# Attention scores of the last three query tiles: four fp32 quadrant products, or three rounded products with 128 queries as weights

## The chip, the cores and the metric

The program runs on one core of a Trainium2 chip. The metric is device time in microseconds (us), the median of several executions; one further execution was recorded by the hardware profiler, and all rows below come from that one.

## The reference

Talking-heads attention feeds two dense two-layer networks, all in fp32. The part that the change touches is the product of queries and keys in the second line.

```python
B, H, S, D = 2, 12, 448, 64
scores = 0.125 * q @ k.T                               # per batch and head, 448 x 448
scores = einsum('bhij,hg->bgij', scores, w_pre)        # heads mixed before the softmax
scores = scores - max(scores, -1)
attn = exp(scores); attn = attn / (sum(attn, -1) + 1e-9)
attn = einsum('bhij,hg->bgij', attn, w_post)           # heads mixed after it
x = (attn @ v) as 896 rows of 768
h = x @ w_in;  x = where(h > 0, h, exp(min(h, 0)) - 1) @ w_out
h = x @ w2_in; out = (h * sigmoid(h)) @ w2_out
```

## The kernel before

**Scores.** The 896 query rows of both batches stand in seven tiles of 128 rows (T = 0 to 6). For a tile and a pair of heads p (0 to 5), `qk_pair(T, p)` on PE multiplies queries `qt` (64 partitions for the even head, 64 for the odd one) with keys `kt`. It issues four products, one for each quadrant of the array: head e of the pair picks the rows of the array, half c of the queries picks the columns. Operands are plain fp32, and the trace has two records of a product, each preceded by a weight load. The results lie in two PSUM banks (`pq`, tags qk0 and qk1), one for each head. `qk_evac` scales them into `s`, the even head on ACT and the odd one on DVE.

**Steps.** Attention then runs in 45 hand-ordered steps (`step(s)`). A step mixes heads for 20 query rows: DMAs on SP bring score rows into `blk` (three buffers, two steps ahead); PE makes `pre` from it (`premix`, quadrants of 64x64); DVE takes the row maximum `nmx`; ACT makes `pe` by an exponential with row sums; DVE inverts the sums; POOL scales the second mixing matrix by them into `krn` (`recip`); and in the step after, PE makes `post` (`postmix`, quadrants again), which ACT and DVE copy into `a`. PE's order in a step is `pre`, then in some steps two pairs of `av` (attention times values, 128 rows by 64 columns of the array), then one pair of scores `pq`, then `post` of the step before. Steps with `av` are called long here, the others short. Tables (`QK_AT`, `X_AT`, `D_AT`, `A_AT`, `M_AT`, `B_AT`) say in which step and at which place of it further work is issued; every engine works through its queue in the order in which the code issues.

Scores of tile 4 are made in steps 17 to 22, of tile 5 in 23 to 28, of tile 6 in 29 to 34. Of these 18 steps the eight 17, 19, 21, 25, 27, 29, 31 and 33 are short and the other ten long. Step 17 begins at 66.61 us of the trace, step 18 at 68.93, step 19 at 73.21, step 28 at 103.51, step 29 at 108.69, step 35 at 128.54.

**Weights of the first network** are already prepared in these steps: the table `EARLY` gives for four half chunks the steps of load, `scale_w` (ACT), two bit operations `bits_w` (DVE), the rounding `split_hi` (ACT, a cast to fp32r) and the remainder `split_lo` (DVE). The two networks follow from about 160 us on: every factor there is split into a rounded part (fp32r) and a remainder, and a product is made of three rounded products, high by high, high by low, low by high, with 128x128 weights and 448 columns.

Of the kernel before, what the change touches and what calls it, by code (L numbers as in the profile page):

```python
# [7 lines left out]
F32 = mybir.dt.float32  # L8
F32R = mybir.dt.float32r
# [4 lines left out]
ALU = mybir.AluOpType  # L14
# [3 lines left out]
P = 128  # L18
B, H, S, D = 2, 12, 448, 64
# [3 lines left out]
NP = H // 2  # L23
# [5 lines left out]
HS = 64  # L29
# [6 lines left out]
KO = (0, 2, 4, 1, 3, 5)  # L36
AHEAD = 2
KS = 10
OUT2 = ((0,), (1,), (2,), (0, 1), (3,), (2, 3), (4,), (5,), (4, 5))
KB = -(-S // BI)  # L40

# [37 lines left out]
def attn_moe_moe(ctx: ExitStack, tc: tile.TileContext, q, k, v, w_pre, w_post, w1i, w1o, w2i, w2o, out):  # L79
    nc = tc.nc  # L80
# [3 lines left out]
    def pool(name, **kw):  # L84
        cm = tc.tile_pool(name=name, reuse_waits="tile", **kw)
        return cm, cm.__enter__()

    cm_c, cp = pool("const", bufs=1, side="left")
    cm_k, kp = pool("kt", bufs=1, side="right")
    cm_al, al = pool("align", bufs=1, side="right")  # L90
    al.tile([P, 40], F32, name="align")
    cm_w, wp = pool("qt", bufs=1, side="right")
# [17 lines left out]
        return min(TI, S - t * TI)  # L110

    NQ = len(QTILES)
    qT, kT = {}, {}

    def load_q(T, eng=None, parts=(slice(0, NP),)):
        if T not in qT:
            qT[T] = wp.tile([P, NP, 2 * P], F32, name=f"qt{T}", tag="qT", bufs=3).rearrange("p a b -> p (a b)")[:, :NP * P].rearrange("p (a b) -> p a b", a=NP)
        for p in parts:
            (eng or nc.sync).dma_start(qT[T][:, p], q[T, :, p])

    def load_k(b, p, eng=nc.sync):
        if b == 0:
            kT[p] = kp.tile([P, 2, S], F32, name=f"kt{p}", tag=f"kT{p}")
        eng.dma_start(kT[p][:, b], k[b, p])  # L124

    def load_v(b, g, eng=nc.sync):

# [11 lines left out]
    def qk_pair(T, p, where=("qk0", "qk1")):  # L139

        bs = QTILES[T][1]
        if T not in smap:
            smap[T] = (sp1, sp0, sp2)[T % 3].tile([P, H, S], F32, name=f"s{T}", tag="s")
        pq = [ps.tile([P, S], F32, name=f"pq{T}_{p}_{e}", tag=w, bufs=1) for e, w in enumerate(where)]
        for c in range(2):
            for e in range(2):
                half = slice(e * D, (e + 1) * D)
                nc.tensor.matmul(pq[e][HS * c:HS * c + HS], qT[T][half, p, HS * c:HS * c + HS], kT[p][half, bs[c % len(bs)]], start=True, stop=True, tile_position=(e * D, HS * c))  # L148
        sev.append((T, p, pq))

    def qk_evac(e):
        for T, p, pq in sev:
            o = smap[T][:, 2 * p + e]
            if e == 0:
                nc.scalar.activation(o, pq[0], AF.Copy, scale=0.125)  # L155
            else:
                nc.vector.tensor_scalar(o, pq[1], 0.125, None, op0=ALU.mult)
        if e == 1:
            sev.clear()
# [97 lines left out]
    def av_pair(T, p):  # L257

        b, t = tiles[T]
        m = rows(t)  # L260
        if p % 2 == 0:
            late = T + 1 == len(tiles)
            avt[T] = ps.tile([P, 2, TI], F32, name=f"av{T}_{p}", tag=("pre2", "qk0", "pre0")[p // 2] if late else {(0, 0): "qk0", (0, 2): "qk0", (2, 4): "pre2", (6, 2): "qk0"}.get((T, p), "av"), bufs=1)
        for j in range(4):
            for e in range(2):
                h = 2 * p + e
                nc.tensor.matmul(avt[T][e * D:(e + 1) * D, p % 2, :m], vall[b][:NV, h, j], amap[T][:NV, j * H + h, :m], start=j == 0, stop=j == 3, tile_position=(0, e * D))  # L267
        if p % 2 == 1:
            (xsp if T + 2 >= len(tiles) else xev).append((T, p - 1, m, avt.pop(T)))
# [11 lines left out]
    def av_split():  # L281
        for T, p, m, av in xsp:
            c = slice(tiles[T][1] * TI, tiles[T][1] * TI + m)
            x = x1_tile()
            nc.scalar.copy(x[:, p:p + 2, 0, c], av[:, :, :m])
            nc.scalar.copy(xmap[1][:, p:p + 2, c], av[:, :, :m])
            nc.vector.tensor_tensor(x[:, p:p + 2, 1, c], av[:, :, :m], x[:, p:p + 2, 0, c], op=ALU.subtract)
        xsp.clear()
# [3 lines left out]
    for p in range(NP):  # L292
        load_k(0, p)
        if p < 2:
            load_q(0, nc.scalar, (slice(0, 2), slice(2, NP))[p:p + 1])
# [14 lines left out]
    for p in range(NP):  # L310
        qk_pair(0, p, BANKS[p % 3])
        qk_evac(0)
        qk_evac(1)
    for s in range(AHEAD):
        relayout(s)
    for p in range(LEAD):
        qk_pair(1, p, BANKS[p])
        qk_evac(0)
        qk_evac(1)

    NT_ = len(tiles)
    QK_AT, X_AT, D_AT, A_AT = {}, {}, {}, {}

    def at(d, step, f):
        d.setdefault(int(step), []).append(f)

    for T, n0 in enumerate((-LEAD, 1, 11, 17, 23, 29), 1):
        for p in range(LEAD if T == 1 else 0, NP):
            at(QK_AT, n0 + p, lambda T=T, p=p: qk_pair(T, p))
    for T, st in ((3, 7), (4, 15), (5, 20)):  # L330
        at(D_AT, st, lambda T=T: load_q(T))
    at(A_AT, 26, lambda: load_q(6, nc.scalar))
    AV_AT = (8, 10, 12, 14, 16, 18, 20, 22, 23, 24, 26, 28, 30, 32, 34, 36, 38, 40, 42, 43, 44)
    for T in range(NT_ - 1):
        for p in range(NP):
            at(X_AT, AV_AT[3 * T + p // 2], lambda T=T, p=p: av_pair(T, p))
    for p in range(NP):
        e, st = ((A_AT, 8), (D_AT, 10), (A_AT, 10), (A_AT, 12), (D_AT, 14), (A_AT, 14))[p]
        at(e, st, lambda p=p, e=e: load_k(1, p, nc.scalar if e is A_AT else nc.sync))
    for g, st in ((1, 1), (2, 4), (3, 6)):  # L340
        at(D_AT, st, lambda g=g: load_v(0, g))
    for g in range(4):
        e, st = ((D_AT, 18), (A_AT, 24), (A_AT, 28), (A_AT, 32))[g]
# [38 lines left out]
        run(M_AT, s)  # L382

    M_AT, F_AT, B_AT = {}, {}, {}

    xq = {}

# [14 lines left out]
    def x1_conv(p):  # L402
        c = slice(0, 2 * TI)
        x, t = xmap[1][:, p, c], x1_tile()
        nc.scalar.copy(t[:, p, 0, c], x)
        nc.gpsimd.tensor_tensor(t[:, p, 1, c], x, t[:, p, 0, c], op=ALU.subtract)

    chunks = []
    for w in (w1i, w1o, w2i, w2o):
# [8 lines left out]
        else:  # L418
            for x in OUT2:
                for c in x if len(x) == 2 else x * 2:  # L420
                    chunks.append(("out", w, c, (KS, 6) if len(x) == 2 else ((0, 5), (5, 5))[sum(y[2] == c and y[1] is w for y in chunks)]))

# [23 lines left out]
    def ring(n):  # L446
        if n >= O2:
            n += 2 * sum(x[0] == "out" and x[3][0] == KS and i % 2 == 1 for i, x in enumerate(chunks[O2:n]))
        return (n + 2 * (n >= KF)) % 4
# [62 lines left out]
    def g_op(moe, f, hf, i):  # L512
        return gop[moe, f][i][:, hf]
# [27 lines left out]
    def moe_out(n, moe, c, k0, kn, hfs=(0, 1)):  # L541
# [3 lines left out]
        for hf in hfs:  # L545
            po = state[moe, c][hf]
            n_ = 0
            for wt, gi in ((hi, 0), (hi, 1), (lo, 0)):
                for kk in range(kn):
                    nc.tensor.matmul(po, wt[:, kk * P:(kk + 1) * P], g_op(moe, k0 + kk, hf, gi), start=(k0 == 0 and n_ == 0), stop=(k0 + kn == (KF, KS)[moe] and n_ == 3 * kn - 1))  # L550
                    n_ += 1
# [51 lines left out]
    for p in range(NP):  # L603
        at(M_AT, s6 - 4 + 2 * p, lambda p=p: split_x(p))
        at(M_AT, (39, 41, 42, 42, 43, 44)[p], lambda p=p: x1_conv(p))
    EARLY = ((16, 18, 20, 20, 22, 22), (18, 20, 22, 23, 23, 24), (22, 24, 24, 26, 30, 30), (24, 26, 26, 28, 31, 32))
    for i, (l, sc, b0, b1, h_, lo) in enumerate(EARLY):
        n, j = divmod(i, 2)
        e = (A_AT, D_AT)[i > 2]
# [34 lines left out]
    for g in range(3):  # L644
        for p in range(2 * g, 2 * g + 2):
            av_pair(NT_ - 1, p)
        av_split()
# [35 lines left out]
    h = {}  # L683
# [288 lines left out]
    for t, n_ in zip(x, "B11_0 B11_1 B11_2 T1_0 T1_1 T1_2 B21_0 B21_1 B22_0 T2_0 T2_1 B22_1 T3_0 T3_1 T4_0 T4_1 B21_2 T2_2 T3_2 T4_2 B22_2".split()):  # L972
        a, i = n_.split("_")
        xt[1][a, int(i)] = t
    for n in range(O1 + 8, I2):
# [4 lines left out]
        if po:  # L980
            c = chunks[n][2]
# [11 lines left out]
    for f in range(KF):  # L993
        x = f + 2 if f < KS else f - KS
        raw[1, f] = rt[x // 3][:, x % 3] if x < 9 else rk[x - 9]
    hb[1] = rk[3:]
    x = [ge[u][:, i] for u in range(2) for i in range(3)] + [gs[:, i] for i in range(6)]
    x += [rr[u][:, i] for u in range(2) for i in range(3)]
    for f in range(KS - 1):
        gop[1, f] = x[2 * f:2 * f + 2]  # L1000
# [8 lines left out]
    def gk(*ps):  # L1009
        return [kp.tile([P, 2, S], F32R, name=f"gk{p}", tag=f"kT{p}") for p in ps]  # L1010

    def last_homes():
        gop[1, KS - 1] = gk(3, 5)

# [88 lines left out]
    n = O2 + 1  # L1103
    while n < NCH:
        c, k = chunks[n][2:]
# [4 lines left out]
        i = n - O2  # L1110
# [90 lines left out]
```

## Time and profile before

| | us |
|---|---|
| median of 3 runs | 597.76 (596.16 to 600.27) |
| the profiled execution, its own time | 598.09 |
| its span, first to last instruction | 596.3 |

The profiled execution lies 0.33 us above the median and has 1.8 us outside its span. A row of the timeline gives start, length, engine, line of the kernel, operation, written and read tile, shape and count of instructions merged in it; a bracket tells the idle time just before and what ended it. A matmul's recorded length includes the way through the array, so the time that PE needs for a group is read from start to start.

### The profile page before, as it was taken

The numbers are of one execution on the slowest core, as the hardware profiler recorded it, in microseconds if no ns is written. First come the engines' busy times: TensorE is split into PE (matmuls) and PEld (weight loads), VectorE is DVE, ScalarE is ACT, GpSimd is POOL, SyncE is SP. The second block draws the span as 40 slices with busy tenths as digits, with TensorE's granted clock in tenths as the row PEclk, the third lists the DMA queues.
The fourth block names the chain that finished last, engine by engine and source line by source line (L and its number), as shares of the span: only waits on it lengthen the run. The fifth ranks groups of instructions, "written<-read, shape, count | busy, mean of one in ns | idle before, by whom it ended". The sixth has DMA issues, their size and how long they took to land.

```text
span 596.3 us, 14978 instructions
## 1 busy us (share of the span) xinstructions
PE 586.7 (98%) x6130; PEld 503.2 (84%) x6130; DVE 459.4 (77%) x763; ACT 374.4 (63%) x685; POOL 53.7 (9%) x112
## 2 busy tenths in 40 slices
PE   9989999999999999999999999999999999999997
PEld 3456666666799999999999999999999999999996
DVE  4877888777789999968776764699888879976642
ACT  5777778777757777777864634476766666533311
POOL 1222222346400000000000000000000000000000
PEclk9999999999999999999999999999999999999999
DMA  6666667444423344322253344144334323463601
GB/s 244 232 216 216 194 204 228 161 158 154 127 102 106 124 143 130 117 88 90 93 155 106 103 128 145 66 160 146 119 106 137 103 88 103 136 197 114 202 1 62
DMA packets 37592, 82.04 MB, mean 138 GB/s; under 512 B 4115, under 2 KB 18195, under 8 KB 37523
## 3 DMA queue, kind: packets, MB, share of 16 engines
q1 hardware_dynamic: 35363, 76.87, 39.6%
q10 hardware_dynamic: 2160, 4.21, 2.3%
q8 instruction: 48, 0.79, 0.6%
q14 instruction: 21, 0.17, 0.1%
HBM read 59.05 MB, written 2.75 MB: 104 GB/s over the span
## 4 chain that ended last, share of the span: by engine, by line
PE 95%; DVE 1%; ACT 1%; DMA 1%; issue 1%; POOL 0%; SPq 0%; DVEq 0%; ACTq 0%; POOLq 0%
PE b L812 32%; PE po L550 31%; PE post L239 6%; PE av L267 6%; PE pre L196 5%; PE pq L148 5%; PE q L1050 4%; PE ph L536 3%; PE po L1050 2%; DMA kt<-in_k_dram 1%; ACT pe L214 1%; DVE nmx L202 1%; POOL krn L227 0%; SPq L124 0%; DVE a L134 0%
## 5 line engine op out<-in xcount | busy, mean ns | idle before, releaser
L812 PE MATMUL b<-x,we 128*128 128x448 f32 x396 | 101.1, 362 | 0.0
L812 PEld LDWEIGHTS b<-x,we 128*128 128x128 f32 x396 | 74.3, 188 | 4.9
L214 ACT ACTIVATE pe<-pre,nmx 124x448 f32<-124x448 f32 x90 | 56.4, 632 | 26.1 <-DVE nmx L202 19.7
L812 PE MATMUL b<-rr,we 128*128 128x448 f32 x288 | 69.5, 362 | 0.0
L739 ACT ACTIVATE wr<-wr 128x768 f32<-128x768 f32 (+1 forms) x63 | 54.6, 867 | 19.1 <-DMA wr<-in_w1o_dram 8.4
L239 PEld LDWEIGHTS post<-krn,pe 60*64 60x64 f32 x2520 | 45.0, 135 | 22.7 <-POOL krn L227 11.3
L735 DVE SCALAR_TENSOR_TENSOR wc<-wr,wc 128x768 int32<-128x768 int32 (+1 forms) x64 | 58.1, 908 | 3.8 <-ACT wr L739 0.4
L550 PE MATMUL po<-ge,we 128*128 128x448 f32 x216 | 60.3, 362 | 0.0
L550 PE MATMUL po<-gs,we 128*128 128x448 f32 x216 | 59.9, 362 | 0.0
L812 PEld LDWEIGHTS b<-rr,we 128*128 128x128 f32 x288 | 54.1, 188 | 3.5
L202 DVE TENSOR_REDUCE nmx<-pre 124x1 f32<-124x448 f32 x90 | 51.8, 614 | 4.2 <-PE pre L196 2.9
L550 PE MATMUL po<-x,we 128*128 128x448 f32 x192 | 50.1, 362 | 0.0
L267 PEld LDWEIGHTS av<-a,v 128*64 128x64 f32 x768 | 36.9, 137 | 15.6 <-ACT pe L214 5.6
L508 DVE TENSOR_TENSOR we<-wc,we 128x640 fp32r<-128x640 f32 (+1 forms) x30 | 25.8, 859 | 30.6 <-ACT we L499 30.6
L239 PE MATMUL post<-krn,pe 60*64 60x60 f32 x2520 | 46.9, 219 | 2.1 <-POOL krn L227 1.6
L196 PE MATMUL pre<-blk,kpre 64*64 64x448 f32 (+1 forms) x360 | 46.6, 541 | 1.1 <-issue 1.1
L227 POOL TENSOR_SCALAR krn<-kps,sum 124x60 f32<-124x60 f32 x90 | 37.8, 435 | 103.8 <-DVE sum L223 71.9
L550 PE MATMUL po<-ta,we 128*128 128x448 f32 x168 | 44.8, 362 | 0.0
L719 ACT CAST we<-wc 128x768 fp32r<-128x768 f32 (+1 forms) x36 | 30.0, 833 | 21.4 <-PE b L812 13.1
L550 PEld LDWEIGHTS po<-ge,we 128*128 128x128 f32 x216 | 40.6, 188 | 2.6
L550 PEld LDWEIGHTS po<-gs,we 128*128 128x128 f32 x216 | 40.6, 188 | 2.6
L148 PE MATMUL pq<-kt,qt 64*64 64x448 f32 x336 | 41.1, 557 | 1.2 <-ACT s L155 0.8
(149 smaller groups left out, 1069.5 us busy)
## 6 DMA issues: line engine op xcount, KB each, us to landing
blk<-s SPq DMA_DIRECT2D x77, 210.0 KB
wr<-in_w2i_dram SPq DMA_DIRECT2D x32, 384.0 KB
wr<-in_w1i_dram SPq DMA_DIRECT2D x29, 384.0 KB
wr<-in_w1o_dram SPq DMA_DIRECT2D x24, 384.0 KB
wr<-in_w2o_dram SPq DMA_DIRECT2D x24, 384.0 KB
wr<-in_w1o_dram SPq DMA_DIRECT2D x12, 256.0 KB
wr<-in_w2o_dram SPq DMA_DIRECT2D x12, 256.0 KB
qt<-in_q_dram SPq DMA_DIRECT2D x5, 384.0 KB
```

The lines of the kernel that those rows point to most:

```text
L148: nc.tensor.matmul(pq[e][HS * c:HS * c + HS], qT[T][half, p, HS * c:HS * c + HS], kT[p][half, bs[c % len(bs)]], start=True, stop=True, til ...
L196: nc.tensor.matmul(pre[s][r][HS * c:HS * c + HS], kpre[o], blkb[o, s % NBUF, c], start=True, stop=True, tile_position=(HS * r, HS * c))
L202: nc.vector.tensor_reduce(nmx[s][:n, r:r + 1], pre[s][r][:n], axis=AX.X, op=ALU.max, negate=True)
L214: nc.scalar.activation(t[:n], pre[s][r][:n], AF.Exp, bias=nmx[s][:n, r:r + 1], scale=1.0, accum_out=sums[s][:n, r:r + 1])
L227: nc.gpsimd.tensor_scalar(t[:n], kps[:n], z[:n, r:r + 1], None, op0=ALU.mult)
L239: nc.tensor.matmul(w[c][HS * u:HS * u + HS, r, j * BW:(j + 1) * BW], pexp[s][r][o, m * HS:(m + 1) * HS], kr[s][r][o].rearrange("p h i -> p ...
L267: nc.tensor.matmul(avt[T][e * D:(e + 1) * D, p % 2, :m], vall[b][:NV, h, j], amap[T][:NV, j * H + h, :m], start=j == 0, stop=j == 3, tile_ ...
L550: nc.tensor.matmul(po, wt[:, kk * P:(kk + 1) * P], g_op(moe, k0 + kk, hf, gi), start=(k0 == 0 and n_ == 0), stop=(k0 + kn == (KF, KS)[moe] ...
L735: nc.vector.scalar_tensor_tensor(cc, r[:, :, 1], 3, cc, op0=ALU.logical_shift_left, op1=ALU.bitwise_or)
L739: nc.scalar.activation(hf, hf, AF.Prelu, scale=2.0 ** -112, alpha=2.0 ** 32)
L812: nc.tensor.matmul(o, wt[:, u * KH + i * P:u * KH + (i + 1) * P], X[x, i][:, xi], start=start and n_ == 0, stop=n_ == 8, skip_group_check= ...
L1050: nc.tensor.matmul(o, wt[:, u * KH + i * P:u * KH + (i + 1) * P], t[i][:, xi] if x == "B22" else t[:, i, xi], start=start and n_ == 0, sto ...
```

## The change

For tiles 4 to 6 (`T >= TS`, with `TS = 4`) `qk_pair` uses split operands. Keys of batch 1 land in a tile of their own (`k1`) and not in the second half of `kt`. When a pair's last product with `kt` is through, its buffer is taken over by `ks`: POOL rounds the keys to fp32r (`k_hi`) and subtracts (`k_lo`). Of the queries ACT makes the rounded part (`q_hi`, all six pairs at once) and POOL the remainder in two halves (`q_lo`). A pair of scores is then three accumulating rounded products for each head, with 64 rows and 128 columns of the array. Queries of tile 4 are loaded in step 12 and not 15, and `EARLY` moves some preparation of weights to later steps.

```diff
+TS = 4
...
+        if T >= TS:
+            for n, (i, j) in enumerate(((0, 0), (0, 1), (1, 0))):
+                for e in range(2):
+                    half = slice(e * D, (e + 1) * D)
+                    nc.tensor.matmul(pq[e], qs[T][half, i, p], ks[p][half, j], start=n == 0, stop=n == 2, tile_position=(e * D, 0), skip_group_check=True)
+        else:
+            for c in range(2):
+                for e in range(2):
+                    half = slice(e * D, (e + 1) * D)
+                    nc.tensor.matmul(pq[e][HS * c:HS * c + HS], qT[T][half, p, HS * c:HS * c + HS], kT[p][bs[c % len(bs)]][half], start=True, stop=True, tile_position=(e * D, HS * c))
...
+    def k_hi(p):
+        ks[p] = kp.tile([P, 2, S], F32R, name=f"ks{p}", tag=f"kT{p}")
+        nc.gpsimd.tensor_copy(ks[p][:, 0], kT[p][1])
+
+    def k_lo(p):
+        nc.gpsimd.tensor_tensor(ks[p][:, 1], kT[p][1], ks[p][:, 0], op=ALU.subtract)
+
+    def q_hi(T):
+        qs[T] = wp.tile([P, 2, NP, P], F32R, name=f"qs{T}", tag="qT", bufs=3)
+        nc.scalar.copy(qs[T][:, 0], qT[T])
+
+    def q_lo(T, i):
+        h = slice(3 * i, 3 * i + 3)
+        nc.gpsimd.tensor_tensor(qs[T][:, 1, h], qT[T][:, h], qs[T][:, 0, h], op=ALU.subtract)
...
-    for T, st in ((3, 7), (4, 15), (5, 20)):
+    for T, st in ((3, 7), (4, 12), (5, 20)):
...
+    for p in range(NP):
+        at(M_AT, (11, 12, 14, 15, 16, 18)[p], lambda p=p: k_hi(p))
+        at(M_AT, (12, 13, 14, 16, 17, 18)[p], lambda p=p: k_lo(p))
+    for T, h, l in ((4, 14, (15, 16)), (5, 21, (22, 22)), (6, 27, (28, 28))):
+        at(M_AT, h, lambda T=T: q_hi(T))
+        for i in range(2):
+            at(M_AT, l[i], lambda T=T, i=i: q_lo(T, i))
...
-    EARLY = ((16, 18, 20, 20, 22, 22), (18, 20, 22, 23, 23, 24), (22, 24, 24, 26, 30, 30), (24, 26, 26, 28, 31, 32))
+    EARLY = ((16, 18, 20, 20, 29, 30), (18, 20, 22, 23, 29, 30), (22, 24, 31, 31, 33, 34), (24, 26, 32, 33, 34, 36))
```

In the rows of order below, the number behind a tile's name is that of the step, or of the tile and the pair, and the last one a running number of the buffer. PE in step 19, before, where the third pair of tile 4 stands between `pre` of step 19 and `post` of step 18:

```order
L196 MATMUL pre19_0_1442<-blk_94,kpre_89 64x448
L196 MATMUL pre19_1_1443<-blk_94,kpre_89 64x448
L148 MATMUL pq4_2_0_1448<-kt2_105,qt4_1215 64x448
L148 MATMUL pq4_2_1_1449<-kt2_105,qt4_1215 64x448
L148 MATMUL pq4_2_0_1448<-kt2_105,qt4_1215 64x448
L148 MATMUL pq4_2_1_1449<-kt2_105,qt4_1215 64x448
L239 MATMUL post0_95<-krn18_0_1427,pe18_0_1421 64x60
```

The same place with the change:

```order
L207 MATMUL pre19_0_1469<-blk_94,kpre_89 64x448
L207 MATMUL pre19_1_1470<-blk_94,kpre_89 64x448
L154 MATMUL pq4_2_0_1475<-ks2_1164,qs4_1167 128x448
L154 MATMUL pq4_2_1_1476<-ks2_1164,qs4_1167 128x448
L154 MATMUL pq4_2_0_1475<-ks2_1164,qs4_1167 128x448
L154 MATMUL pq4_2_1_1476<-ks2_1164,qs4_1167 128x448
L154 MATMUL pq4_2_0_1475<-ks2_1164,qs4_1167 128x448
L154 MATMUL pq4_2_1_1476<-ks2_1164,qs4_1167 128x448
L250 MATMUL post0_95<-krn18_0_1451,pe18_0_1445 64x60
```

Four products with 64 output rows became six with 128; nothing else moves on PE.

ACT's queue at the end of step 27 (evacuation `s` of a pair, copy `a`, exponentials `pe` of step 28), before:

```order
L155 ACTIVATE s5_1757<-pq5_4_0_2053 128x448
L132 COPY a4_1811<-post0_95 128x2x48x5
L214 ACTIVATE pe28_0_2168,sum28_2167<-pre28_0_2107,nmx28_2164 124x448
L214 ACTIVATE pe28_1_2170,sum28_2167<-pre28_1_2108,nmx28_2164 124x448
L278 COPY xr0_741<-av3_4_2113 128x2x88
```

and with the change:

```order
L166 ACTIVATE s5_1793<-pq5_4_0_2090 128x448
L137 COPY a4_1849<-post0_95 128x2x48x5
L341 CAST qs6_2146<-qt6_2075 128x768
L225 ACTIVATE pe28_0_2211,sum28_2210<-pre28_0_2148,nmx28_2207 124x448
L225 ACTIVATE pe28_1_2213,sum28_2210<-pre28_1_2149,nmx28_2207 124x448
```

The rounding of the queries of tile 6 now stands ahead of the exponentials of step 28.

POOL's queue in steps 28 and 29, before:

```order
L227 TENSOR_SCALAR krn28_0_2175<-kps_90,sum28_2167 124x60
L227 TENSOR_SCALAR krn28_1_2177<-kps_90,sum28_2167 124x60
L227 TENSOR_SCALAR krn29_0_2243<-kps_90,sum29_2231 124x60
L227 TENSOR_SCALAR krn29_1_2245<-kps_90,sum29_2231 124x60
L227 TENSOR_SCALAR krn30_0_2321<-kps_90,sum30_2313 124x60
```

and with the change:

```order
L238 TENSOR_SCALAR krn28_0_2217<-kps_90,sum28_2210 124x60
L238 TENSOR_SCALAR krn28_1_2219<-kps_90,sum28_2210 124x60
L345 TENSOR_TENSOR qs6_2146<-qt6_2075,qs6_2146 128x384 x2
L238 TENSOR_SCALAR krn29_0_2289<-kps_90,sum29_2277 124x60
L238 TENSOR_SCALAR krn29_1_2291<-kps_90,sum29_2277 124x60
```

The two halves of the remainder of tile 6 stand behind `krn` of step 28 and ahead of that of step 29, the step in which PE uses them first.

## Rows read from the trace of the kernel before

**Rows 1.** The page: span, busy time of engines, the chain that ended last.

```profile
span 596.3 us, 14978 instructions
PE 586.7 (98%) x6130; PEld 503.2 (84%) x6130; DVE 459.4 (77%) x763; ACT 374.4 (63%) x685; POOL 53.7 (9%) x112
...
PE 95%; DVE 1%; ACT 1%; DMA 1%; issue 1%; POOL 0%; SPq 0%; DVEq 0%; ACTq 0%; POOLq 0%
```

**Rows 2.** Stages: length, then PE, PEld, DVE, ACT, POOL busy, clock, DMA.

```profile
66.61:86.76 20.15, 20.15 (x541) 13.46 (x536) 17.27 (x41) 16.50 (x43) 4.87 (x13) 1.00 0.65 199
86.76:108.69 21.93, 21.18 (x573) 14.18 (x568) 17.91 (x43) 16.70 (x43) 4.90 (x13) 1.00 0.66 206
108.69:128.54 19.85, 19.85 (x542) 13.38 (x536) 16.30 (x39) 15.81 (x41) 8.36 (x17) 1.00 0.51 181
175.00:596.00 421.00, 417.22 (x2087) 391.32 (x2085) 324.80 (x455) 247.53 (x363) 0.00 (x0) 1.00 0.36 116
```

**Rows 3.** Timeline of PE, steps 17 to 19 (start, length, what).

```profile
66.61 0.94 PE L196 MATMUL pre<-blk,kpre 64*64 64x448 f32 x8
67.37 0.93 PE L148 MATMUL pq<-kt,qt 64*64 64x448 f32 x8
68.12 0.99 PE L239 MATMUL post<-krn,pe 60*64 60x60 f32 x56
68.93 0.94 PE L196 MATMUL pre<-blk,kpre 64*64 64x448 f32 x8
69.80 1.86 PE L267 MATMUL av<-a,v 128*64 128x120 f32 x32
71.59 0.98 PE L148 MATMUL pq<-kt,qt 64*64 64x448 f32 x8
72.40 0.99 PE L239 MATMUL post<-krn,pe 60*64 60x60 f32 x56
73.21 0.94 PE L196 MATMUL pre<-blk,kpre 64*64 64x448 f32 x8
73.97 0.93 PE L148 MATMUL pq<-kt,qt 64*64 64x448 f32 x8
```

**Rows 4.** Timeline of PE where quadrants and full-array rounded products alternate.

```profile
157.38 1.04 PE L239 MATMUL post<-krn,pe 60*64 60x60 f32 x56
158.35 1.49 PE L536 MATMUL ph<-x,we 128*128 128x448 f32 x6
159.76 1.04 PE L239 MATMUL post<-krn,pe 60*64 60x60 f32 x56
```

**Rows 5.** Timeline of PE at the start of step 28.

```profile
103.51 0.54 PE L196 MATMUL pre<-blk,kpre 64*64 64x448 f32 x1
104.80 0.98 PE L196 MATMUL pre<-blk,kpre 64*64 64x448 f32 x7 [0.75 <-issue]
```

**Rows 6.** Groups by line and form: count, busy us and mean ns, idle before.

```profile
L391 POOL TENSOR_TENSOR x<-xr,x 128x448 fp32r<-128x448 f32 x6 | 6.8, 1140 | 0.4
...
L499 ACT CAST we<-wc 128x768 fp32r<-128x768 f32 x8 | 6.6, 830 | 6.8 <-DVE wc L735 6.6 <-DVE wc L487 0.2
...
L390 POOL CAST x<-xr 128x448 fp32r<-128x448 f32 x5 | 2.8, 558 | 0.0
```

**Rows 7.** Timeline of POOL and ACT, steps 17 and 18.

```profile
70.03 0.65 ACT L132 COPY a<-post 128x480 f32<-128x480 f32 x1
...
70.37 0.84 POOL L227 TENSOR_SCALAR krn<-kps,sum 124x60 f32<-124x60 f32 x2 [3.31 <-DVE sum L223]
...
72.83 0.84 POOL L227 TENSOR_SCALAR krn<-kps,sum 124x60 f32<-124x60 f32 x2 [1.61 <-DVE sum L223]
```

**Rows 8.** Groups of weight preparation on DVE, 45 to 165 us.

```profile
L487 DVE SCALAR_TENSOR_TENSOR wc<-wr,wc 128x384 int32<-128x384 int32 x6 | 3.5, 583 | 0.4 <-ACT wr L465 0.2
...
L505 DVE TENSOR_TENSOR we<-wc,we 128x384 fp32r<-128x384 f32 x4 | 2.2, 548 | 0.0
L485 DVE TENSOR_SCALAR wc<-wr 128x384 int32<-128x384 int32 x6 | 2.1, 349 | 0.0
```

More of the change, by code (lines that the diff above doesn't have):

```diff
@@ L112, in attn_moe_moe @@
     NQ = len(QTILES)
-    qT, kT = {}, {}
+    qT, kT, kr1, qs, ks = {}, {}, [], {}, {}
     def load_q(T, eng=None, parts=(slice(0, NP),)):
@@ L122, in load_k @@
         if b == 0:
-            kT[p] = kp.tile([P, 2, S], F32, name=f"kt{p}", tag=f"kT{p}")
-        eng.dma_start(kT[p][:, b], k[b, p])
+            kT[p] = [kp.tile([P, 2, S], F32, name=f"kt{p}", tag=f"kT{p}")[:, 0]]
+        else:
+            if not kr1:
+                kr1.append(cp.tile([P, NP, S], F32, name="k1", tag="xr1"))
+            kT[p].append(kr1[0][:, p])
+        eng.dma_start(kT[p][b], k[b, p])
     def load_v(b, g, eng=nc.sync):
@@ L144, in qk_pair @@
         pq = [ps.tile([P, S], F32, name=f"pq{T}_{p}_{e}", tag=w, bufs=1) for e, w in enumerate(where)]
[L145 to L148, printed above, removed]
+        if T >= TS:
[3 more added lines that the diff above has]
+                    nc.tensor.matmul(pq[e], qs[T][half, i, p], ks[p][half, j], start=n == 0, stop=n == 2, tile_position=(e * D, 0), skip_group_check=True)
+        else:
+            for c in range(2):
+                for e in range(2):
+                    half = slice(e * D, (e + 1) * D)
+                    nc.tensor.matmul(pq[e][HS * c:HS * c + HS], qT[T][half, p, HS * c:HS * c + HS], kT[p][bs[c % len(bs)]][half], start=True, stop=True, tile_position=(e * D, HS * c))
         sev.append((T, p, pq))
```

## The prediction

> **What bounds the kernel now.** I read the page first, then the stages, then PE's timeline inside a step. On the page PE is busy for 98% of the span, and 95% of the chain that ended last lies on it [rows 1]. Busy time of PE flatters it, because a matmul's record runs on while the next has begun, so the stages have to confirm it. In the 421 us from 175 to 596 PE has 2087 rounded matmuls in 417.22 us, 0.20 us each, without a gap to speak of [rows 2]: nothing ahead of that stretch changes its length, and the change does not touch it. The whole effect lies in the 61.9 us of steps 17 to 34, where PE is busy for 20.15 of 20.15, 21.18 of 21.93 and 19.85 of 19.85 us, and DVE for 82 to 86% [rows 2]. In the timeline of these steps the groups follow each other at fixed distances: from `pre` to `pq` 0.76 us (66.61 to 67.37), from `pq` to `post` 0.75, from `post` to `pre` 0.81 [rows 3]. PE sets the step; DVE is the next one behind it.
>
> **A pair of scores on PE.** Today it takes 0.75 us in a short step [rows 3]. With the change it is three rounded products deep, if the two heads run side by side. A rounded product of 448 columns takes 0.20 us [rows 2], so 3 x 0.20 = 0.60. That the two heads run side by side is seen today: four products of 448 columns in four passes take 0.75, which is 0.42 ns for a column and pass, and one product alone would need that. The two row halves thus already share their time, with 64 columns of the array each; with 128 columns no row shows it. Taken at this, a pair gains 0.15 us, 18 pairs 2.7 us.
>
> **The change of array shape.** Against this stands something that the fixed distances show. Where PE goes from one shape of the array to another, time is lost. In step 18 `pre` (64x64) to `av` (128x64) takes 0.87 and not 0.76 us [rows 3]; `av` should take 16 places x 120 columns x 2 passes x 0.42 ns = 1.61 and takes 1.79; and the pair behind it 0.81 (71.59 to 72.40) and not 0.75. That is 0.11 + 0.18 + 0.06 = 0.35 us for the two changes around `av`. A second place gives the same: `post` and six rounded full-array products, 157.38 to 159.76, take 2.38 us [rows 4]; at 0.81 and 6 x 0.20 they would take 2.01, so 0.37 for a change in and one out. I take 0.36 for two, 0.18 for one. In both places the rows or the whole array change; a change from 64x64 to 64x128, which moves only the column split, stands in no row. Its price is between 0 and these 0.18; I take 0.18, since at both seen places the next weights came only after the array had run empty, and here too weights of one shape must follow those of another.
>
> In a short step the pair stands between two quadrant groups: two changes more, 0.60 + 0.36 - 0.75 = +0.21 us, eight times, +1.7. In a long step `av` ahead of it had to be left anyway: one change more, 0.60 + 0.18 - 0.75 = +0.03, ten times, +0.3. Sum on PE: **+2.0 us**; without any price of a change it is -2.7.
>
> A sentence apart: the Trainium skill, "TensorEngine Tiling (Array Packing)", section "Tiling Modes", says that changing the tiling mode, not just the tile, drains the engine, and lists 64x64 and 64x128 as two modes. By that rule the sum is the +2.0, and without it the -2.7. The trace agrees with the rule where it shows a change (0.35 and 0.37 us for two), and shows no change of columns alone.
>
> **POOL.** It gets six roundings of keys (0.56 each), six remainders (1.14) and six half remainders of queries of 384 columns, for which I scale 1.14 by 384/448 to 0.98 [rows 6]; 16 us in all. They stand behind `krn` of their step and ahead of the next one. POOL waits 3.3 us ahead of the `krn` of odd steps and 1.6 ahead of that of even ones in this stretch (one of each in [rows 7]). The tables put at most 0.56 + 1.14 + 0.98 = 2.7 into the former (step 16) and 0.56 + 0.98 = 1.54 into the latter (step 15). All fit; cost 0. If they did not, `krn` would have to be later than `post` wants it: in step 18 it ends at 73.67, and `post` starts 0.75 after 73.97, at 74.72, so 1.05 us are free.
>
> **The start of tile 6.** Here the cover is thin. `q_hi` (0.83 for 768 columns [rows 6]) stands on ACT at the end of short step 27 between the copy `a` and the exponentials of step 28; `q_lo` stands behind `krn` of step 28; and PE wants it in step 29. Read from the like steps 17 to 19: the copy ends at 70.68, exponentials follow 0.1 later, so they slip by about 0.8; `krn`, at 72.83 to 73.67, slips to 74.5; the half remainder ends at 75.45; PE reaches the third product at 73.97 + 0.2 for the shape + 0.4 = 74.6. That is a wait of 0.85 us, once; its lower end is 0. For tile 4 a step lies between, and for tile 5 ACT loses a rounding of weights at the same place and step 23 has `av` ahead of the pair, so 0 there.
>
> **The stop in step 28.** PE stands from 103.51 to 104.80 with one `pre` matmul issued, and the releaser reads "issue" [rows 5]: no engine and no data is named. These 1.3 us may be there again or not, as the stream of instructions is shorter by four records a pair. If it stays, it covers the wait for `q_lo`, sum 0; if it goes, -1.3 + 0.85 = -0.45. I take the middle, -0.2.
>
> **DVE and ACT.** In steps 29 to 34 DVE gains two shifts of 0.35, two merges of 0.58 and one remainder of 0.55 [rows 8], 2.4 us: 16.3 becomes 18.7 in 19.85 us. That is tight, and a late maximum or reciprocal eats into the 1.05 us above. ACT gains 0.83 us in each of steps 14, 21 and 27 and has 20.15 - 16.50 = 3.65 us free in the first of the three stages, more in the second [rows 2]. Bounds: 0, and 1.5 us if half of the 2.4 and a part of the ACT work come through. I take +0.3, near 0, since the 1.05 us cover any single one of these. The queries of tile 4 that load three steps earlier cost 0; what would uncover them is a wait of `pre` for `blk`.
>
> **The sum.** +2.0 + 0 - 0.2 + 0.3 = +2.1. Against the profiled execution 598.09 + 2.1 = 600.2; this lies 0.33 above the median of the runs, so for the median **599.9 us**.
>
> **Rivals.**
> - *The shape costs nothing* when only the columns are split otherwise. For it: the row halves stay. Against: both seen kinds of change cost 0.18. -2.7 - 0.2 + 0.3 = -2.6, so 595.2.
> - *The two heads do not run side by side* with 128 columns each (or a rounded product needs the two passes of a full one). Then a pair takes 1.2 us and not 0.6, 18 x 0.6 = 10.8 more: 610.7. For it: no row shows two products that are 128 columns wide at once. Against: quadrants above each other share the same columns today and lose nothing. It decides as soon as the pair exceeds 0.75 us by more than the shape costs.
> - *DVE becomes the bound* in steps 29 to 34. For it: 18.7 us of work in 19.85. If it cannot be busier than today's largest share, 17.27 of 20.15 or 0.86, it needs 21.8 us there, and at the 0.82 of that stage itself 22.8, where PE with the change needs 19.85 + 0.7 = 20.6: +1.2 to +2.2, so up to 602.1. Against: it waits for PE and ACT today and can move up.
> - *The change does not do what it says* (still full products): the order shows six rows of 128 columns for four of 64, so I leave it no chance beyond what the second rival holds.
>
> **How the numbers follow.** Forecast 0.62, free shape 0.21, no sharing 0.09, DVE 0.08. The range takes in the forecast's own ends (599.9 less 1 for the stop gone and no other wait, plus 1.5) and the free shape with its ends, and the DVE case: 594.0 to 603.5, leaving out the no-sharing case and edges, about 0.15. Within 1% (591.8 to 603.7, about what a measurement here can tell from no change) lie the first two and most of the fourth: 0.87. Slower by over 1%: 0.11. Faster by over 1% would need 6 us, and all pairs at 0.15 bring 2.7: 0.02.
>
> **What would show it.** In a short step: `pre` to `pq` 0.87 and not 0.76, `pq` to `post` near 0.8, `post` to `pre` 0.86, the step 2.5 and not 2.32 us; a long one as today. For the free shape: 0.76, 0.60, 0.81, step 2.17. For no sharing: `pq` to `post` over 1.2. Step 29: a wait of PE for POOL `qs` of up to 0.85. Step 28: no stop of 1.3 ahead of `pre`, or it stands elsewhere. POOL's `krn` in step 16 within 0.1 of its place. The prediction would be wrong above all if a change of columns alone drains nothing, or drains more than at the seen places because two weight loads of 128 columns stand exposed.

## The result and the profile after

| | before | after |
|---|---|---|
| median, us (16 runs each) | 597.49 | 601.05 |
| lowest and highest | 596.16 to 600.27 | 599.06 to 603.69 |
| the profiled execution, its own time | 598.09 | 600.05 |
| its span | 596.3 | 598.3 |

The ratio of after to before is 1.0055, with a 95% interval of 1.0039 to 1.0071: 3.3 us slower, at least 2.3 and at most 4.2. The forecast was 599.9 us, 2.1 more than the median known then, a little under the lowest end of that interval; its range of 594.0 to 603.5 us holds the measured median.

The page of the changed kernel, the lines that answer to [rows 1]:

```profile
span 598.3 us, 14913 instructions
...
PE 589.4 (99%) x6094; PEld 505.0 (84%) x6094; DVE 460.6 (77%) x763; ACT 375.6 (63%) x688; POOL 69.3 (12%) x130
...
PE 94%; ACT 2%; DVE 2%; POOL 1%; issue 1%; DVEq 0%; ACTq 0%; POOLq 0%
```

PE has 36 records fewer and is busy 2.7 us longer; POOL has 15.6 us more, about the 16 that were counted for it. PE is still nearly the whole chain. The stages that answer to the first three of [rows 2], now steps 17 to 22, 23 to 28 and 29 to 34 (length, then PE, PEld, DVE, ACT, POOL busy, clock, DMA):

```profile
66.58:87.19 20.61, 20.61 (x530) 13.95 (x524) 16.73 (x40) 16.68 (x43) 10.33 (x19) 1.00 0.67 201
87.19:108.44 21.25, 21.25 (x562) 14.55 (x556) 16.22 (x38) 16.55 (x43) 6.75 (x14) 1.00 0.64 210
108.44:129.87 21.43, 20.98 (x529) 14.01 (x524) 18.27 (x44) 16.05 (x43) 10.26 (x19) 1.00 0.47 165
```

Together they take 63.29 us, where those of [rows 2] sum to 61.93. The granted clock is full in all of them, so what they lost they lost in their steps. The first step before them begins at 66.58 (before 66.61), and from the start of step 44 to the end it is 441.6 us in either trace, so the networks behind did not change. Between the two lie steps 35 to 43, to which the table `EARLY` moves a part of the preparation of weights: 26.76 us, before 26.16. The timeline of PE in steps 17 to 19, as in [rows 3]:

```profile
66.58 0.94 PE L207 MATMUL pre<-blk,kpre 64*64 64x448 f32 x8
67.45 0.87 PE L154 MATMUL pq<-ks,qs 64*128 64x448 f32 x6
68.24 1.04 PE L250 MATMUL post<-krn,pe 60*64 60x60 f32 x56
69.11 0.94 PE L207 MATMUL pre<-blk,kpre 64*64 64x448 f32 x8
69.97 1.86 PE L278 MATMUL av<-a,v 128*64 128x120 f32 x32
71.76 0.88 PE L154 MATMUL pq<-ks,qs 64*128 64x448 f32 x6
72.58 1.04 PE L250 MATMUL post<-krn,pe 60*64 60x60 f32 x56
73.44 0.94 PE L207 MATMUL pre<-blk,kpre 64*64 64x448 f32 x8
74.30 0.88 PE L154 MATMUL pq<-ks,qs 64*128 64x448 f32 x6
```

Read from start to start: `pre` to `pq` is 0.87 (0.76 before), `pq` to `post` 0.79 to 0.82 (0.75), `post` to `pre` 0.87 (0.81). A short step takes 2.53 and not 2.32 us, a long one 4.33 and not 4.28. The short step has the distances that the prediction gave for a paid change of shape, to a few hundredths; the long one is 0.05 longer, where it gave one as today. The start of step 28, where [rows 5] have the stop, and step 29, where tile 6 begins:

```profile
104.46 0.94 PE L207 MATMUL pre<-blk,kpre 64*64 64x448 f32 x8
105.33 1.50 PE L278 MATMUL av<-a,v 128*64 128x88 f32 x32
...
108.44 0.94 PE L207 MATMUL pre<-blk,kpre 64*64 64x448 f32 x8
109.30 0.68 PE L154 MATMUL pq<-ks,qs 64*128 64x448 f32 x4
110.43 0.47 PE L154 MATMUL pq<-ks,qs 64*128 64x448 f32 x2 [0.45 <-POOL qs L345]
110.82 1.04 PE L250 MATMUL post<-krn,pe 60*64 60x60 f32 x56
```

The stop is gone: the eight `pre` are one row, and `av` follows at 0.87. In step 29 PE has done four of its six products and waits for the remainder of the queries; the step lasts 3.25 us, 0.71 more than a short one. POOL at that place:

```profile
108.57 0.84 POOL L238 TENSOR_SCALAR krn<-kps,sum 124x60 f32<-124x60 f32 x2 [1.87 <-ACT s L166]
109.37 1.96 POOL L345 TENSOR_TENSOR qs<-qt,qs 128x384 fp32r<-128x384 f32 x2
```

`krn` comes first and the remainder behind it, as the order said; each half of it takes 1.00 us, the first ends at 110.37, and PE goes on at 110.43. The groups of POOL's new work (mean ns behind the busy time), beside [rows 6]:

```profile
L337 POOL TENSOR_TENSOR ks<-k,ks 128x448 fp32r<-128x448 f32 x6 | 6.9, 1142 | 0.2
...
L345 POOL TENSOR_TENSOR qs<-qt,qs 128x384 fp32r<-128x384 f32 x6 | 5.9, 1003 | 0.0
L334 POOL CAST ks<-k 128x448 fp32r<-128x448 f32 x6 | 3.3, 558 | 0.0
```

### The profile page after: what moved, and what is told of

The parts are those of the page before. It is cut to its first block, busy times and chain, and to the rows that moved or that the text cites. A ratio compares the mean times of both kernels' runs of the same rounds, so it can differ in the third digit from the quotient of the medians.

```text
span 598.3 us, 14913 instructions
## 1 busy us (share of the span) xinstructions
PE 589.4 (99%) x6094; PEld 505.0 (84%) x6094; DVE 460.6 (77%) x763; ACT 375.6 (63%) x688; POOL 69.3 (12%) x130
## 4 chain that ended last, share of the span: by engine, by line
PE 94%; ACT 2%; DVE 2%; POOL 1%; issue 1%; DVEq 0%; ACTq 0%; POOLq 0%
PE b L845 32%; PE po L583 31%; PE post L250 6%; PE av L278 6%; PE pre L207 5%; PE q L1083 4%; PE pq L159 3%; PE ph L569 3%; PE po L1083 2%; PE pq L154 2%; ACT pe L225 1%; DVE nmx L213 1%; POOL krn L238 1%; PE warm L319 1%; ACT a L137 0%
## 5 line engine op out<-in xcount | busy, mean ns | idle before, releaser
L250 PEld LDWEIGHTS post<-krn,pe 60*64 60x64 f32 x2520 | 43.2, 134 | 20.2 <-POOL krn L238 11.3
L207 PE MATMUL pre<-blk,kpre 64*64 64x448 f32 x360 | 46.1, 541 | 0.4 <-issue 0.4
L278 PE MATMUL av<-a,v 128*64 128x120 f32 (+1 forms) x768 | 41.7, 262 | 0.2 <-ACT a L137 0.2
```

The lines of the kernel that those rows point to most:

```text
L207: nc.tensor.matmul(pre[s][r][HS * c:HS * c + HS], kpre[o], blkb[o, s % NBUF, c], start=True, stop=True, tile_position=(HS * r, HS * c))
L250: nc.tensor.matmul(w[c][HS * u:HS * u + HS, r, j * BW:(j + 1) * BW], pexp[s][r][o, m * HS:(m + 1) * HS], kr[s][r][o].rearrange("p h i -> p ...
```

## The experiments

Theory: the change of array shape around the pair costs PE what the pair itself does not gain back, and the first step of tile 6 waits for POOL. Rivals: the later places of weight preparation cost it (DVE or ACT), or the stops named "issue" do, by the number of PE's records. All ratios are to the kernel before on the same chip, with 95% intervals.

**The kernel before once more, unchanged** (its trace, one execution).

> The kernel before once more, unchanged, for a second profile. If the stop of PE at the start of step 28 (103.51 to 104.80) belongs to that one execution, this profile has none there and a span near 595 us. If it belongs to the program, PE stops at the same matmul for about 1.3 us again and the span is near 596.3.

596.19 us, span 594.4. The starts of step 20 and of step 28 in the timeline of PE, the latter up to `av`:

```profile
79.66 0.98 PE L196 MATMUL pre<-blk,kpre 64*64 64x448 f32 x8 [0.41 <-issue]
...
102.98 0.94 PE L196 MATMUL pre<-blk,kpre 64*64 64x448 f32 x8
103.86 1.43 PE L267 MATMUL av<-a,v 128*64 128x88 f32 x32
```

The stop of [rows 5] is not in this execution; step 28 takes 3.85 us here and 5.18 there. Another one stands in step 20, which takes 4.87 and not 4.28. So not every execution of the kernel has the stop of step 28. Steps 17 to 34 take 60.81 us here, with 0.6 of that for the stop in step 20; this trace, and not the 61.93 of the first, is the better one to hold the change against.

**The shape alone**: the kernel before, with its plain fp32 operands, but 128 queries as weights in tiles 4 to 6. No splits, no new work for POOL, ACT or DVE, the weights as before.

```diff
-        for c in range(2):
+        if T >= 4:
             for e in range(2):
                 half = slice(e * D, (e + 1) * D)
-                nc.tensor.matmul(pq[e][HS * c:HS * c + HS], qT[T][half, p, HS * c:HS * c + HS], kT[p][half, bs[c % len(bs)]], start=True, stop=True, tile_position=(e * D, HS * c))
+                nc.tensor.matmul(pq[e], qT[T][half, p], kT[p][half, bs[0]], start=True, stop=True, tile_position=(e * D, 0))
```

> The kernel before, with nothing but the shape of the products of tiles 4 to 6 changed: two full fp32 products of 128 queries for a pair and not four of 64. Theory (the change of array shape costs): pre to pq 0.87 us and not 0.76, post to pre 0.86 and not 0.81, a short step 2.32 + 0.37 = 2.69, a long one 0.18 more, in all 8 x 0.37 + 10 x 0.18 = +4.8 us. Rival (rounded products of 64 rows are slower than 0.20 us or share their time badly, and the shape is free): no change of any distance, within 1 us of the kernel before.

601.21 us, ratio 1.0064 [1.0035, 1.0092]; span 599.0, 4.6 above that of the kernel before beside it. The timeline of PE, steps 17 to 19:

```profile
65.88 0.94 PE L201 MATMUL pre<-blk,kpre 64*64 64x448 f32 x8
66.74 1.02 PE L148 MATMUL pq<-kt,qt 64*128 64x448 f32 x4
67.69 1.04 PE L244 MATMUL post<-krn,pe 60*64 60x60 f32 x56
68.56 0.94 PE L201 MATMUL pre<-blk,kpre 64*64 64x448 f32 x8
69.42 1.86 PE L272 MATMUL av<-a,v 128*64 128x120 f32 x32
71.22 1.02 PE L148 MATMUL pq<-kt,qt 64*128 64x448 f32 x4
72.17 1.04 PE L244 MATMUL post<-krn,pe 60*64 60x60 f32 x56
73.03 0.94 PE L201 MATMUL pre<-blk,kpre 64*64 64x448 f32 x8
```

The same work in the other shape: 2.68 in place of 2.32 for the short step, 0.36 more; 4.47 in place of 4.28 for the long one, 0.19 more. A change of columns alone costs what the changes of rows and of the whole array cost in the kernel before. The weight loads (PEld) of step 17 show where it goes, first in the kernel before, then in this one (a bracket here is idle time of the loads alone):

```profile
66.99 0.15 PEld L148 LDWEIGHTS pq<-kt,qt 64*64 64x64 f32 x4 [0.22 <-issue]
...
67.75 0.16 PEld L239 LDWEIGHTS post<-krn,pe 60*64 60x64 f32 x4 [0.22 <-issue]
```

```profile
66.74 0.30 PEld L148 LDWEIGHTS pq<-kt,qt 64*128 64x128 f32 x4 [0.71 <-issue]
67.69 0.21 PEld L244 LDWEIGHTS post<-krn,pe 60*64 60x64 f32 x8 [0.65 <-issue]
```

In the kernel before the loads start 0.38 and 0.37 us ahead of the first products of `pq` (67.37) and `post` (68.12) [rows 3], while the products of the group before are running. Here they start together with their own products, at 66.74 and 67.69. The loads of `post` are as wide as before and lose their lead too, so it is not only the wider weights of 128 queries that stand exposed, which the prediction had named as a danger. The run also parts the change's two effects: the shape costs 0.36, and three rounded products in place of a plain one give 0.14 back (2.68 to 2.54).

**No change of shape**: the changed kernel with its three products in quadrants. The operands are split into two parts of 16 bits (F16) here and in all quadrant kernels below, so these differ from the changed kernel in the operand format as well as in the shape.

```diff
-                for e in range(2):
+                for c in range(2):
+                    for e in range(2):
...
-        ks[p] = kp.tile([P, 2, S], F32R, name=f"ks{p}", tag=f"kT{p}")
+        ks[p] = kp.tile([P, 2, S], F16, name=f"ks{p}", tag=f"kT{p}")
...
-        qs[T] = wp.tile([P, 2, NP, P], F32R, name=f"qs{T}", tag="qT", bufs=3)
+        qs[T] = wp.tile([P, 2, NP, P], F16, name=f"qs{T}", tag="qT", bufs=3)
```

> The changed kernel with split operands of 16 bits (fp16 high and remainder) and the three products as four quadrants of 64x64 each, so that PE keeps one shape from pre through pq to post; all other work as in the changed kernel. Theory (shape): pre to pq 0.76, pq to post 0.60, post to pre 0.81, a short step 2.17, the 18 pairs 2.7 us less than before, with the wait for the remainder of tile 6 of up to 0.9 us still there: about 2 us faster than before, 5 faster than the changed kernel. Rival (the splitting on POOL and ACT and the moved preparation of weights cost the time): slower than before by 1 us or more although the pairs are shorter.

599.75 us, ratio 1.0031 [0.9997, 1.0065]. In the steps the theory held: `pre` to `pq` 0.76, `pq` to `post` 0.57, `post` to `pre` 0.81, a short step 2.14 and a long one 4.06 where nothing disturbs them. In the time it did not: steps 17 to 34 take 60.86 us, no less than the 60.81 above. Some 3.6 us (8 x 0.18 and 10 x 0.22) were gained in the distances and lost again between them: 1.06 in step 29 (3.20 and not 2.14), most of it for POOL's remainder as in the changed kernel, 0.36 for ACT in step 32, and stops of 0.54 and 0.30 in steps 19 and 28.

**Queries of tile 6 earlier**: the changed kernel, with these loaded in step 24, rounded in 26, their remainder in 27 and 28.

```diff
-    at(A_AT, 26, lambda: load_q(6, nc.scalar))
+    at(A_AT, 24, lambda: load_q(6, nc.scalar))
...
-    for T, h, l in ((4, 14, (15, 16)), (5, 21, (22, 22)), (6, 27, (28, 28))):
+    for T, h, l in ((4, 14, (15, 16)), (5, 21, (22, 22)), (6, 26, (27, 28))):
```

> The changed kernel with the queries of tile 6 loaded in step 24 and not 26, rounded by ACT at the end of step 26 and not 27, their remainders on POOL in steps 27 and 28. Theory: the wait of PE in step 29 for POOL (0.75 us, 109.30 to 110.43 against 0.40 for two products) goes and nothing takes its place: 0.7 us less than the changed kernel, some 2.5 above the kernel before. Rival: the exponentials of step 27 or 28 or krn become late instead and PE waits as long elsewhere.

600.36 us, ratio 1.0041 [1.0019, 1.0063], span 597.2. Step 29 in the timeline of PE:

```profile
107.97 0.94 PE L207 MATMUL pre<-blk,kpre 64*64 64x448 f32 x8
108.83 0.88 PE L154 MATMUL pq<-ks,qs 64*128 64x448 f32 x6
109.64 1.04 PE L250 MATMUL post<-krn,pe 60*64 60x60 f32 x56
110.51 0.94 PE L207 MATMUL pre<-blk,kpre 64*64 64x448 f32 x8
```

The six products are in one piece and the step takes 2.54 us. The wait was real and worth its 0.71 in the trace; the ratio went down by 0.0014, 0.8 us, which the intervals alone could not tell.

**The changed kernel once more, unchanged** (its trace, one execution).

> The changed kernel once more, unchanged, for a second profile. Shape theory: short steps of 2.54 and long ones of 4.34 us again, the wait for POOL in step 29 again (0.7 us), and stops of PE that are put down to issue, if any, at other places than in its first profile. If the time were lost in chance stops alone, the step distances would differ between the two profiles.

600.6 us, span 598.8. Short steps 2.53 to 2.59, long ones 4.33 to 4.39 (3.90 to 4.03 where `av` has 88 columns), step 29 3.33 with its wait; steps 17 to 34 take 63.52 (63.29 in the first trace). No stop named "issue" between steps 17 and 34 in either.

**Quadrants with the earlier queries**: the third kernel with the edit of the fourth.

> The kernel with 16-bit split operands in quadrants, and the queries of tile 6 loaded, rounded and split a step or two earlier. Theory: the wait of PE in step 29 (0.9 us) goes, short steps 2.14 and long ones 4.06 where nothing stops PE, so 0.9 us less than with the late queries, near the time of the kernel before or 1 us under it. Rival: stops and waits of the other engines take the gain again, and the time stays 1 to 2 us above the kernel before.

598.62 us, ratio 1.0020 [0.9991, 1.0048]. Step 29 takes 2.18, its wait is gone, but steps 20 and 22 take 5.75 and 5.04 where 4.06 would do, with stops of 1.40 and 0.61 named "issue". Steps 17 to 34 come to 60.88.

**The later places of weight preparation alone**: the kernel before with the changed table `EARLY`.

```diff
-    EARLY = ((16, 18, 20, 20, 22, 22), (18, 20, 22, 23, 23, 24), (22, 24, 24, 26, 30, 30), (24, 26, 26, 28, 31, 32))
+    EARLY = ((16, 18, 20, 20, 29, 30), (18, 20, 22, 23, 29, 30), (22, 24, 31, 31, 33, 34), (24, 26, 32, 33, 34, 36))
```

> The kernel before with nothing but the moved preparation of weights (the changed table EARLY). Theory: PE sets the step and DVE keeps up, so no change beyond 0.5 us; the wait ahead of av in step 20 (0.35 to 0.6 us) may go or stay. Rival (DVE becomes the bound in steps 29 to 34): +1.2 to +2.2 us, with steps 30 to 34 longer than 4.28 and 2.32.

598.33 us, ratio 1.0005 [0.9981, 1.0029], so between 1.1 us faster and 1.7 slower: no change that can be told. Its trace has one stop in steps 17 to 34:

```profile
106.42 0.98 PE L196 MATMUL pre<-blk,kpre 64*64 64x448 f32 x7 [2.43 <-issue]
```

It stands in step 28 between the first `pre` and the other seven, the very place of [rows 5], and PE idles three times as long as there (2.43 and 0.75 us).

**More records of PE**: the kernel before with each product of tiles 4 to 6 cut into two of 224 columns, 16 for a pair and not 8.

```diff
+        for x in (slice(0, S // 2), slice(S // 2, S)) if T >= 4 else (slice(0, S),):
```

> The kernel before with each product of tiles 4 to 6 issued as two of 224 columns: the same streaming and the same shape, twice the PE instructions of a pair (32 records and not 16). Theory (stops named issue come from the supply of instructions to PE): the distances inside a step stay at 0.76, 0.75 to 0.78 and 0.81, but stops named issue appear more often, and the time is 1 us or more above the kernel before. Rival (they are chance, or belong to transfers of data): no stop more than before and no change of time beyond 0.5 us.

597.90 us, ratio 1.0005 [0.9981, 1.0029]; short steps 2.33, long ones 4.28, one stop of 1.44 in step 22. Twice the records of a pair cost nothing that can be told, and the trace has no more stops. This is a weak test of the thought that the stops come from the supply of instructions: the 288 additional records are a small part of PE's stream, and where the one stop stands speaks for that thought (last section).

**Quadrants, queries of tiles 5 and 6 earlier, weights at their old places.** The split queries lie in the unused half of the buffer of the queries, so that tile 5 can load in step 15 and be split in 18 and 20.

> 16-bit split operands in quadrants, the queries of tiles 5 and 6 prepared earlier, their split parts kept in the idle half of the buffer of the queries, and with that the preparation of weights back at the steps of the kernel before. Theory (with the shape kept and DVE relieved in steps 29 to 34, PE sets the step): short steps 2.14 and long ones 4.06 to 4.2 in steps 17 to 34, no wait for POOL, 3 us less than the kernel before in these steps where no chance stop falls, and a median 1 to 3 us under the kernel before. Rival (with shorter steps PE runs into its supply of instructions or into ACT): stops named issue and waits take 2 us or more again and the median is no better than the kernel before.

597.19 us, ratio 0.9972 [0.9949, 0.9995], for the first time below the kernel before.

**The sixth kernel once more, unchanged** (its trace, one execution).

> The 16-bit quadrants with the early queries of tile 6 once more, for a second profile. If stops of PE are chance, they stand in other steps than in its first profile (20 and 22 there, 2.7 us together); steps 30 to 32, which were 0.2 to 0.4 us longer than the shortest, are so again if DVE is what holds them.

598.79 us, span 597.0; steps 17 to 34 take 61.74. The stop in step 20 is back at the same instruction, ahead of the last 13 of `post`:

```profile
80.06 0.40 PE L251 MATMUL post<-krn,pe 60*64 60x60 f32 x13 [1.84 <-issue]
```

**The ninth kernel again, and with the late weights**, side by side, to tell a gain of the old places from a lucky measurement.

> The same kernel as in the ninth run, measured again beside the kernel with the late table. If its gain of 0.28% was the kernel's and not that run's, the ratio lies between 0.995 and 1.000, with steps 35 to 43 in 26.2 us as in the kernel before. If it was that run's luck, the ratio lies near 1.002, as for the two quadrant kernels before it.

> The ninth kernel with one edit undone: the weights are prepared at the changed kernel's late places. Theory that the late places cost the quadrant kernels what they lost: the ratio is 0.003 to 0.005 above that of the ninth kernel in the same measurement, steps 30 to 32 take about 4.4, 2.5 and 4.4 us and steps 35 to 43 take 26.5 in place of 26.2. Rival, that the places of weight preparation don't matter (they cost nothing in the kernel before, ratio 1.0005): both kernels come within 0.002 of each other.

598.43 us, ratio 0.9989 [0.9959, 1.002], and 598.07 us, ratio 0.9992 [0.9963, 1.0022]. The gain did not come again, and the two kernels are alike: the rival held. The late places cost 0.3 us in steps 35 to 43 (26.48 against 26.15). The timeline of PE in the former shows both sides of the quadrants' account, a short step of 2.14 us and the stop in step 20:

```profile
67.81 0.94 PE L210 MATMUL pre<-blk,kpre 64*64 64x448 f32 x8
68.57 0.75 PE L157 MATMUL pq<-ks,qt 64*64 64x448 f16 x12
69.14 1.00 PE L253 MATMUL post<-krn,pe 60*64 60x60 f32 x56
69.95 0.94 PE L210 MATMUL pre<-blk,kpre 64*64 64x448 f32 x8
...
81.81 0.40 PE L253 MATMUL post<-krn,pe 60*64 60x60 f32 x13 [1.18 <-issue]
```

In this trace step 20 takes 5.89 where 4.06 would do, and steps 30 to 32 take 11.56 where 10.26 would do (two long, one short): 1.8 and 1.3 us of the 3.6 gained. No kernel here is shown to be faster than the one before; of those with split operands, the quadrants come level with it.

## Why the prediction was right, and which term was off

*The bound.* PE sets the steps before and after, and most of what the change cost is read from PE's distances in steps 17 to 34. That the whole effect lies there was not right: steps 35 to 43 are 0.6 and 0.2 us longer in the two traces of the changed kernel. The range held the free shape as well as the paid one, so the median inside it says little; what bears the prediction out is the distances.

*The pair and the shape.* Right, and shown twice. The changed kernel has the 0.87, 0.8 and 0.86 of the prediction, and the shape alone costs 0.36 in a short step, the value taken from `av` and from [rows 4]. The two heads with 128 columns each do run side by side: from `pq` to `post` six products and their share of the change of shape take 0.81 us, where one head after the other would need 1.2 for the products alone. So the rivals of a free shape and of no sharing are out. Counted from the traces, eight short steps lose 0.22 and ten long ones 0.06, 2.4 us; the forecast had 2.0, with 0.03 for a long step.

A sentence on the page: the Trainium skill, "TensorEngine Tiling (Array Packing)", section "Tiling Modes", says that a change of mode drains the engine and counts 64x64 and 64x128 as two modes; the trace, which showed no such pair before, now agrees, with 0.36 us for the way in and out.

*POOL.* Right: 558, 1142 and 1003 ns for the three kinds, where 560, 1140 and 980 were counted, and no `krn` that PE had to wait for in these steps. `krn` of step 16 starts at 66.36, before 66.23: a little more than the 0.1 us that the prediction allowed, and at no cost.

*The start of tile 6 and the stop in step 28.* Here the term failed. The wait came, 0.71 and 0.79 us in the two traces, near its upper end of 0.85, and for the reason given: the remainder stands behind `krn` of step 28. But the prediction set against it a credit for the stop of [rows 5] and booked the two together as -0.2. The second trace of the kernel before has no stop in step 28, so the 1.3 us are not in every execution; how many of the 16 runs had them no trace can say, and a credit taken from one execution had no footing in the median. Without the credit the forecast's own terms give 2.0 + 0.85 + 0.3 = 3.15, near the 3.3 measured; that is in part luck, as the shape was 0.4 too low and the wait 0.1 too high.

*DVE and ACT.* A loss of the size of the 0.3 came, but not where it was booked. Steps 30 to 34 take 18.19 us in place of 17.53, and 0.62 of the 0.66 are the distances of PE (two short, three long). DVE is busy for 18.27 of 21.43 us in steps 29 to 34, 0.85, and did not become the bound. The time is lost later: steps 35 to 43 take 26.3 to 27.1 us in all eight traces with the late weights, those of the changed kernel among them (26.76 and 26.33), and 26.15 or 26.16 in all six with the weights at their old places. So this much is shown by the traces, though moving the weights alone measured 1.0005; which wait takes it was not followed further.

*The account.* Held against the execution of the kernel before without the big stop, steps 17 to 34 grew by 2.5 and 2.7 us in the two traces of the changed kernel: 2.4 from PE's distances, 0.7 to 0.8 from the wait, less 0.6 because step 20 had its stop in the one and not in the others. With the 0.6 and 0.2 of steps 35 to 43 this makes 3.1 and 2.9, inside the 2.3 to 4.2 of the runs. The spans differ by more, 3.9 and 4.4, because step 17 begins later, at 66.58 and 67.32 where that trace has 65.87; but it begins anywhere from 65.12 to 66.61 in the five traces with the same code ahead of it, so a cost there is neither shown nor excluded.

The stops named "issue" can be read further than their name; the last section does it. Open stays why they come in one execution and not in the next, and a part of what holds steps 30 to 32 of the quadrant kernels: one trace names ACT `xr` for 0.36 us, and in the trace of the ninth kernel again PE stands for 0.31, 0.42 and 0.16 us at places like those of the stops, of the 1.3 us lost.

## What to carry to other kernels

Count a change of TensorE's array shape as work: here 0.36 us for the way in and out, more than the rounded products gained (0.14). A step that keeps one shape was shorter (2.14 us), but what it gained was lost again in stops and waits. A single execution's stop that names no engine and no data is not a term to set against anything: look for it in a second trace of the same kernel first, and count the instructions up to it. And a gain of 0.3% at the edge of its interval, after several kernels were tried, is to be measured once more before it is believed.

## What the runs showed of the hardware that was not expected

The stops named "issue" come and go from execution to execution, but not anywhere: the kernel before and its twin with the late weights have one in step 28 between the same two `pre` (0.75 us idle in [rows 5], 2.43 in the twin), and four traces of two quadrant kernels have one ahead of the same 13 `post` in step 20 (1.40, 1.71, 1.84 and 1.18 us). Their place can be counted. Number the records of PE and of its sequencer (matmuls, weight loads and some semaphore instructions) in order of their start, from 0. The 14 traces have 32 such stops from 20 us on, and in every one the pause lies ahead of a record whose number leaves the remainder 193 when divided by 256: 4801 in step 28, 3521 in step 20. The page of the kernel before lists a DMA queue that carries instructions:

```profile
q8 instruction: 48, 0.79, 0.6%
```

Its packets have 16384 bytes each, and there is about one for 256 of these records: 48 for 12352 here, 49 for the 12640 of the kernel with more records. Count the first packet to the block that starts at record 449, the next to that at 705, and so on. At each of the 32 stops PE goes on 1.3 to 1.7 us after the packet of its block has landed. In step 28 of the kernel before the packet ended at 103.33 and PE went on at 104.80; in the twin it ended at 104.96 and PE went on at 106.42; in the kernel before once more it had ended at 100.94, and there is no stop. From record 705 on, no block in the 14 traces begins sooner than 1.2 us after its packet. So what PE waits for in these stops is, as far as the traces tell, the next block of its own instructions. In the changed kernel the same block begins inside `av` of step 28, 1.45 us after its packet, and PE runs on: the stop was gone from these two traces because the packets came in time, and nothing shows that the change brought this about.

Why a packet starts late in one execution and not in another no row names. The quadrant kernels work through a block soonest, with 152 records of PE and its weight loads in a short step of 2.14 us, where the kernel before has 144 in 2.32 and the changed kernel 140 in 2.53; that this is why they stop more often is argued here and not shown.

Twelve products of 16-bit operands, three deep in four quadrants, need 0.57 us from start to start, 0.42 ns for each of 3 x 448 columns: one pass for a product. Four plain fp32 products, one deep, need 0.75 us, or four such passes.
